# Splitting the seven-bank score visits, pairing the value products and keeping two chunks of x in a gated attention and FFN kernel

## Chip, cores and metric

The kernel runs on one core of one Trainium2 chip. The metric is the device time of one execution in microseconds (us), as the median of the timed runs. A lower time is better.

## What is computed

The program mixes two branches of the same input x (2048 tokens of 512 features, bf16) with a gate for each token. Branch a is attention with 32 heads of 16 features. The tokens are cut into four segments of 512. Inside a segment the attention is causal softmax; across segments each head carries a memory M (16 x 16) and its normaliser z. Branch b is a gated FFN of 1792 hidden features with a ReLU.

```
g = sigmoid((x * gate_w).sum(-1))
q, k, v = x@wq, x@wk, x@wv                     # 32 heads of 16
for s in range(4):                             # segments of 512 tokens
    p     = softmax(q_s k_s^T / 4 + causal mask)
    a_mem = phi(q_s) M / (phi(q_s) z + 1e-6)    # phi(t) = t+1 if t>0 else exp(t)
    o_s   = sigmoid(beta) * a_mem + (1 - sigmoid(beta)) * (p v_s)
    M, z  = M + phi(k_s)^T v_s, z + sum(phi(k_s))
a = concat(o_s) @ wo
b = (relu(x@W_gate) * (x@W_up)) @ W_down
out = g * a + (1 - g) * b
```

## The kernel before

The program is a list of small operations, made by `program`. Each has a name, an engine, the buffers it reads and writes, and a place in the list, its number. Nothing is scheduled on the chip: the table `ORDER` holds, for each of the five engines, the numbers in the order in which that engine issues them, and the string `BANKS` gives each accumulator its PSUM bank (there are eight banks of 512 float32 columns). The class `Sched` walks the table and puts a semaphore wait in front of an operation where one of its inputs, or the last reader of its bank, is on another engine. So each engine runs its own list strictly in order, and an operation that has to wait holds up all that stand behind it on the same engine.

For each segment the lists hold these steps:

- `proj`: the projections. For each of four head groups G (eight heads) and each of q and k, four matmuls over four 128-row slices of the weights are accumulated in one bank; they are issued as two operations of two slices. v is done the same way per 128 tokens. The copies out of PSUM go to VectorE or ScalarE.
- `att`: scores, exponentials, masks, value products. A block of scores is 128 rows (64 keys for each of two heads) by 512 columns; four blocks of a "quad" are made at once by matmuls of 32 rows each in four row strips of the array. A `visit` writes the blocks into PSUM, one bank for each, and ScalarE turns them into exponentials `E` in SBUF (L714); GpSimd clears what lies above the diagonal (L723). `flush` multiplies a finished head group with the values (L753, 64-row and 32-column strips of the array) into two banks, p = 0 and 1, which VectorE transposes (L761, names `tr`), scales and adds to the memory part.
- `mu` and `nd`: the update of the memory and its read-out (L629, L646, names `num`).
- `ffn`: for each of 14 hidden tiles f, gate (`wg`) and up (`wu`) matmuls, four each in two operations (L839), ReLU of the gate bank (L847 or L848, names `relu`), and the product on VectorE (L850).
- `outp`: the down projection and the output projection, accumulated in one bank for each 128 tokens (L876, L869), scaled and stored.

All weights are loaded once at the start, one slice of 128 rows for a DMA, issued by SyncE (SP) in the order of its list. The value weights wv have four slices; the operation `v0_t` for 128 tokens t of segment 0 comes in two halves, the first of which reads slices 0 and 1 and the second slices 2 and 3. In segments 1 to 3 one visit in four takes seven banks: four blocks with one exponential of 2048 columns and three blocks with one of 1536.

Two lines of the kernel say which buffers there are, and where the seven-bank visits start:

```
QTN, EKN, HTN, OTN, XR = 8, 2, 19, 6, 3
SEVEN = [(), (1,), (1,), (1,)]
```

`XR` is the number of 512-token chunks of x kept transposed in SBUF; `load_x(c)` fills slot c % XR. `QTN` counts slots of q, `HTN` tiles of the FFN's hidden layer, and `TNN` (2) the transposed float32 value products.

Of the kernel before, what the change touches and what calls it, by code (L numbers as in the profile page):

```python
# [6 lines left out]
ALU = mybir.AluOpType  # L7
# [6 lines left out]
TNN = 2  # L14
# [7 lines left out]
QTN, EKN, HTN, OTN, XR = 8, 2, 19, 6, 3  # L22
UNITS = [[8] * 18] * 4
SEVEN = [(), (1,), (1,), (1,)]
CORDER = [[(0, 1, 7, 2, 6, 3, 5, 4), (4, 1, 7, 2, 6, 3, 5, 0)] * 2] * 4
BANKS = ("701342567041527365075111110511114561100067000056077557744557776607075650067657567676454604703400205304145400746001111611"
         "222364635647607727657075506750675616500711762307015104015045015405611111671111127063677076765446007057756705650775670756"
         "10704514215041501053452000012000035766457077516654445757740675546175")
ORDER = {k: [int(x) for x in v.split()] for k, v in {
    "pe": """  # L30
# [386 lines left out]
def program(sc, nc, T, PS, A_x, A_wq, A_wk, A_wv, A_wo, A_beta, W_g, W_u, W_d, gate_w, out, NSEG, KT, NF, NT, EPS, SCALE):  # L417
# [16 lines left out]
    def act(fn, occ, **k):  # L434
        return op("act", fn, occ, **k)
# [506 lines left out]
```

## Time and profile before

| what | value |
|---|---|
| median of 3 timed runs | 261.5 us (261.03 to 261.54) |
| profiled execution: span from first to last instruction | 260.0 us |
| profiled execution: time outside its span | not on the page; the timed runs lie 1.0 to 1.5 us above the span |
| TensorE (PE) busy | 252.7 us, 97% |
| ScalarE (ACT), VectorE (DVE), GpSimd (POOL) busy | 188.0, 171.7, 121.2 us |
| granted TensorE clock | 1.000 |
| HBM read, written | 10.14 MB, 2.11 MB |

The span is one execution taken by the hardware profiler. A row of groups gives the line, engine, operation, what is written and read, the count, busy time in us and the mean ns of one instruction, then the idle time of the engine before them and what ended it. A row of the timeline gives the start and the length in us of a merged run of like instructions; SPq rows are issues of DMAs, and their landing is given apart.

### The profile page before, as it was taken

Reading aid. Unit: us, or ns where it says so; the run is one execution under the profiler, and the core shown is the slowest. Engines: PE = TensorE matmul, PEld = TensorE weight load, DVE = VectorE, ACT = ScalarE, POOL = GpSimd, SP = SyncE. Lnnn points to the kernel's source line nnn. Section 1 sums busy time; section 2 is a strip of 40 time slices with the busy share of each in tenths; the row PEclk is TensorE's granted clock in tenths of the full one; section 3 lists DMA queues with packets and bytes.
Section 4 is the critical chain, followed back from the end, with each engine's and each line's share of the span. In section 5 each row is a group of like instructions: output and inputs, shape, how many; then the busy total and the mean of one; then the engine's idle time right before and its main releaser. Section 6 shows DMA issues by size and latency. Waiting matters only on the chain.

```text
span 260.0 us, 6414 instructions
## 1 busy us (share of the span) xinstructions
PE 252.7 (97%) x2621; PEld 115.4 (44%) x2655; DVE 171.7 (66%) x342; ACT 188.0 (72%) x173; POOL 121.2 (47%) x295
## 2 busy tenths in 40 slices
PE   8999999999999999999999999999999999999997
PEld 4433443434444544444544444434444445343544
DVE  2487788778655789777834478677762138875764
ACT  4598898988778788987777666979787685787000
POOL 2014766575736372587402944257620881168100
DMA  6899997115362311422041023100023022100002
GB/s 217 244 297 221 204 171 162 59 61 143 69 151 52 64 26 37 84 42 63 3 126 42 3 42 59 28 0 0 4 45 83 15 28 43 40 4 0 3 3 81
DMA packets 34925, 19.61 MB, mean 75 GB/s; under 512 B 24144, under 2 KB 34256, under 8 KB 34896
## 3 DMA queue, kind: packets, MB, share of 16 engines
q1 hardware_dynamic: 34512, 18.80, 31.5%
q8 instruction: 21, 0.34, 0.6%
q10 hardware_dynamic: 384, 0.40, 0.4%
q14 instruction: 8, 0.07, 0.1%
HBM read 10.14 MB, written 2.11 MB: 47 GB/s over the span
## 4 chain that ended last, share of the span: by engine, by line
PE 97%; issue 2%; DVE 0%
PE ps L839 38%; PE ps L876 19%; PE ps L589 11%; PE ps L703 9%; PE ps L753 7%; PE ps L587 5%; PE ps L869 5%; PE ps L646 1%; PE ps L506 1%; PE ps L629 1%; PE ps L518 0%; PE ps L527 0%; DVE osb L884 0%
## 5 line engine op out<-in xcount | busy, mean ns | idle before, releaser
L714 ACT ACTIVATE E<-ps 128x2048 bf16<-128x2048 f32 (+1 forms) x75 | 134.3, 1808 | 35.0 <-PE ps L703 34.9
L723 POOL TENSOR_SCALAR_AFFINE_SELECT E<-E 128x256 bf16<-128x256 bf16 (+1 forms) x256 | 100.9, 422 | 103.7 <-ACT E L714 90.3
L839 PE MATMUL ps<-xT,wg 128*128 128x512 bf16 x216 | 58.7, 380 | 1.1 <-issue 0.6
L839 PE MATMUL ps<-xT,wu 128*128 128x512 bf16 x213 | 57.4, 380 | 1.6 <-issue 1.6
L876 PE MATMUL ps<-wd,hT 128*128 128x512 bf16 (+2 forms) x231 | 52.7, 366 | 0.9 <-issue 0.8
L850 DVE TENSOR_TENSOR hT<-ps,rl 128x512 bf16<-128x512 f32 x56 | 37.9, 681 | 14.7 <-PE ps L839 14.2
L876 PEld LDWEIGHTS ps<-wd,hT 128*128 128x128 bf16 x238 | 21.7, 98 | 25.0 <-issue 2.5
L839 PEld LDWEIGHTS ps<-xT,wu 128*128 128x128 bf16 x224 | 20.0, 98 | 25.5 <-issue 3.9
L839 PEld LDWEIGHTS ps<-xT,wg 128*128 128x128 bf16 x224 | 20.2, 98 | 24.5 <-issue 2.8
L884 DVE TENSOR_SCALAR osb<-ps,omg 128x512 bf16<-128x512 f32 (+2 forms) x15 | 10.6, 715 | 27.9 <-PE ps L869 23.9
L703 PE MATMUL ps<-qT,kp 32*128 32x512 bf16 (+7 forms) x512 | 27.6, 286 | 0.0
L761 DVE STREAM_TRANSPOSE Tn<-ps 128x512 f32<-128x512 f32 x32 | 21.4, 699 | 8.3 <-PE ps L753 8.2
L848 DVE TENSOR_SCALAR rl<-ps 128x512 bf16<-128x512 f32 x27 | 18.3, 684 | 9.3 <-PE ps L839 9.2
L847 ACT ACTIVATE rl<-ps 128x512 bf16<-128x512 f32 x29 | 17.1, 595 | 6.7 <-PE ps L839 6.7
L703 PEld LDWEIGHTS ps<-qT,kp 32*128 32x128 bf16 x512 | 9.1, 92 | 24.9 <-ACT E L714 9.3
L753 PE MATMUL ps<-E,vaug 64*17 64x128 bf16 (+7 forms) x512 | 18.6, 283 | 0.0
L753 PE MATMUL ps<-E,vsh 64*17 64x128 bf16 (+7 forms) x512 | 18.2, 283 | 0.0
L770 POOL TENSOR_TENSOR adT<-Tn,rdg 128x512 bf16<-128x512 f32 x12 | 12.7, 1055 | 11.7 <-DVE rdg L768 8.8
L587 PE MATMUL ps<-wv,xT 128*128 128x512 bf16 x60 | 16.6, 379 | 0.6 <-issue 0.6
L589 PE MATMUL ps<-xT,wk 128*128 128x512 bf16 x62 | 16.8, 379 | 0.1
L869 PE MATMUL ps<-wo,oT 128*128 128x512 bf16 (+2 forms) x67 | 16.1, 366 | 0.1
L589 PE MATMUL ps<-xT,wq 128*128 128x512 bf16 (+2 forms) x67 | 15.9, 367 | 0.2 <-issue 0.2
(70 smaller groups left out, 215.8 us busy)
## 6 DMA issues: line engine op xcount, KB each, us to landing
vsh<-vaug SPq DMA_DIRECT2D x8, 272.0 KB, 3.2
out_dram<-osb SPq DMA_DIRECT2D x15, 128.0 KB, 1.9
wg<-in_B_W_gate_dram SPq DMA_DIRECT2D x8, 224.0 KB, 6.1
wu<-in_B_W_up_dram SPq DMA_DIRECT2D x8, 224.0 KB, 5.2
osb<-in_A_x_dram SPq DMA_DIRECT2D x14, 128.0 KB, 3.0
wd<-in_B_W_down_dram SPq DMA_DIRECT2D x7, 256.0 KB, 3.4
wk<-in_A_wk_dram SPq DMA_DIRECT2D x4, 128.0 KB, 3.6
wv<-in_A_wv_dram SPq DMA_DIRECT2D x4, 128.0 KB, 3.6
```

The source lines that it names most:

```text
L587: ins = e.matmul(A(ep)[:, :], lhsT=V.xT[:, kt, tok + col * 128:tok + (col + 1) * 128], rhs=w[:, kt, :], start=(kt == 0), stop=(kt == KT - 1))
L589: ins = e.matmul(A(ep)[:, c0:c1], lhsT=w[:, kt, col * 128:(col + 1) * 128], rhs=V.xT[:, kt, tok + c0:tok + c1], start=(kt == 0 and c0 == 0 ...
L703: ins = q.matmul(PS[:, ep.bank + i, o:o + w], lhsT=V.kp[r, kslot(s, G), c, :], rhs=V.qT[r, qslot(s, G), q0:q0 + w], start=True, stop=True, ...
L714: return a.activation(V.E[:, n * 512:(n + k) * 512].rearrange("q (b n) -> q b n", n=512), PS[:, x.bank:x.bank + k, :], ACT.Exp, scale=SCALE)
L723: pool(lambda g, ap=ap, lim=lim: g.affine_select(out=ap, in_=ap, compare_op=ALU.is_ge, fill=0.0, base=lim, pattern=[[0, 4], [1, 64]], chan ...
L753: ins = q.matmul(A(eps[p])[32 * jj:32 * jj + 17, 64 * (c + u):64 * (c + u + n)], lhsT=v[:, 8 * G + 2 * jj + p, :], rhs=V.E[r, f:f + 64 * n ...
L761: dve(lambda e, p=p, ep=eps[p]: e.transpose(V.Tn[:, 2 * (G % (TNN // 2)) + p, :], A(ep)[:, :]), 709, writes=[f"Tn{2 * (G % (TNN // 2)) + p ...
L839: ins = e.matmul(A(ep)[:, :], lhsT=w[:, kt, f * 128:(f + 1) * 128], rhs=V.xT[:, kt, c % XR * 512:(c % XR + 1) * 512], start=(kt == 0), sto ...
L848: ("dve", lambda e, ep=eg, r=r: e.tensor_scalar(V.rl[:, r, :], A(ep)[:, :], 0.0, None, ALU.max), t_dve(512))],
L850: dve(lambda e, ep=eu, r=r, hs=hs: e.tensor_tensor(V.hT[:, hs, :], A(ep)[:, :], V.rl[:, r, :], ALU.mult), t_dve(512), reads=[f"rl{r}"], wr ...
L869: ins = e.matmul(A(ep)[:, 0:c1 - c0], lhsT=V.oT[:, ot[G], i * 128:(i + 1) * 128], rhs=V.wo[:, G, c0:c1], start=st_ and G == 0, stop=sp_ an ...
L876: ins = e.matmul(A(ep)[:, 0:c1 - c0], lhsT=V.hT[:, slots[f], i * 128:(i + 1) * 128], rhs=V.wd[:, f, c0:c1], start=st_ and f == f0, stop=sp ...
```

## The change

The constants, the buffers and the code of the visits change, and the whole table of orders and banks is another one.

```diff
-TNN = 2
+TNN = 4
-QTN, EKN, HTN, OTN, XR = 8, 2, 19, 6, 3
+QTN, EKN, HTN, OTN, XR = 6, 2, 22, 6, 2
-SEVEN = [(), (1,), (1,), (1,)]
+SEVEN = [(), (2,), (2,), (2,)]
+PAIR = (0, 9)
...
     "sp": """
-4 5 8 9 10 11 12 13 14 15 16 17 18 27 20 19 21 24 22 23 94 26 39 25 92 32 28 31 38 167 40 36 102 37 43 35 29 30 166 33 44 100 34 211 212 104 53 101
+4 5 8 9 10 11 12 13 14 15 17 18 27 20 19 16 24 21 22 90 26 23 39 25 32 88 31 38 50 28 40 98 163 37 30 29 162 35 49 33 47 34 96 45 36 208 207 44 42
...
-        ("braw", [128, 32], BF16), ("eb", [128, 32], F32), ...
+        ("eb", [128, 32], F32), ...
-        ... ("gl", [128, NT], F32), ("tq", [128, 32], BF16),
-        ("rden", [128, 64], F32), ("rdg", [128, 64], F32), ("rdm", [128, 128], F32), ...
+        ("rden", [128, 64], F32), ("rdg", [128, 64], F32), ("rdm", [128, 64], F32), ...
...
-        def visit(groups):
+        def visit(rows, cut):
+            groups = [rows[:cut], rows[cut:]] if cut else [rows]
...
-                    visits.append([[(k + 2 * i, j) for j in range(4)], rows[3 * i:3 * i + 3]])
+                    visits.append(([(k + 2 * i, j) for j in range(4)], 2))
+                    visits.append((rows[3 * i:3 * i + 3], 0))
...
-            while carry and all(left.get(x) == 0 for x in carry[0][3]):
+            while len(carry) > 1 and k in PAIR and all(left.get(x) == 0 for c in carry[:2] for x in c[3]):
+                flush()
                 flush()
```

- A seven-bank visit becomes two operations that stand next to each other on PE. The first writes four banks, and its exponential is cut into two of 1024 columns (two accumulators of two banks). The second writes three banks, with one exponential of 1536 columns. There are 75 visits in place of 63, and 87 exponentials in place of 75.
- A head group's value product is held back until the next group is finished too, and both are created together; four buffers for the transposed products in place of two.
- x keeps two chunks on chip, so that chunks 2 and 3 are loaded into the slots of chunks 0 and 1 after the last matmul that reads those.
- The raw beta is loaded into the first columns of Mbd16, the gate's sums go into gexp, and the read-out of the memory has two buffers for its denominators in place of four.

Lines from 450 on move by 2 to 5: L450 becomes L452, L587 L589, L589 L591, L629 L631, L646 L648, L703 L706, L753 L756, L839 L844, L876 L881.

The orders differ nearly everywhere. Three places follow. The first is the start of the program, on SP, which issues the loads. Numbers 15 to 18 of its table are the slices 0 to 3 of wv, 27 is the gate's weight row gwb, 19 to 22 are slices 0 to 3 of the first half of wg and 23 to 26 those of wu. A row stands for one issue or a run of like ones, and the bracket names the semaphore that SP waits for before it, here that of an earlier load which used the same semaphore. SP before, from the loads of wv on:

```order
L450 DMA wv<-in_A_wv_dram 128x512 x4
L450 DMA gwb<-in_gate_w_dram 128x512 [waits s_dma1]
L450 DMA wg<-in_B_W_gate_dram 128x896 [waits s_dma3]
L450 DMA wg<-in_B_W_gate_dram 128x896 [waits s_dma4]
L450 DMA wg<-in_B_W_gate_dram 128x896 [waits s_dma5]
L450 DMA wu<-in_B_W_up_dram 128x896 [waits s_dma6]
```

SP of the change, from the same place:

```order
L452 DMA wv<-in_A_wv_dram 128x512 x3
L452 DMA gwb<-in_gate_w_dram 128x512
L452 DMA wg<-in_B_W_gate_dram 128x896 [waits s_dma0]
L452 DMA wg<-in_B_W_gate_dram 128x896 [waits s_dma2]
L452 DMA wv<-in_A_wv_dram 128x512 [waits s_dma4]
L452 DMA wu<-in_B_W_up_dram 128x896 [waits s_dma5]
```

Slice 1 of wv moved from the second to the seventh place, behind gwb and the first two slices of wg; the other six keep their order.

On PE the first matmuls that read wv stand at another place too. PE before, from the first scores' neighbourhood (L589 with wk are the k projections, L587 those of v, L703 the scores, L839 the gate):

```order
L587 MATMUL ps<-wv,xT 128x512 [waits s_dma11,s_dma12,s_act]
L587 MATMUL ps<-wv,xT 128x512
L589 MATMUL ps<-xT,wk 128x512 x2
L587 MATMUL ps<-wv,xT 128x512 [waits s_dma13,s_dma15]
L587 MATMUL ps<-wv,xT 128x512
L589 MATMUL ps<-xT,wk 128x512 x4
L703 MATMUL ps<-qT,kp 128x512 [waits s_dve,s_act]
L703 MATMUL ps<-qT,kp 128x512 x3
L587 MATMUL ps<-wv,xT 128x512 x2
L589 MATMUL ps<-xT,wk 128x512 x2
L587 MATMUL ps<-wv,xT 128x512 x2
L839 MATMUL ps<-xT,wg 128x512 [waits s_dma3,s_dma4,s_dve]
```

PE of the change, at the same stage:

```order
L591 MATMUL ps<-xT,wq 128x512
L706 MATMUL ps<-qT,kp 128x512 [waits s_dve,s_act]
L706 MATMUL ps<-qT,kp 128x512 x3
L589 MATMUL ps<-wv,xT 128x512 [waits s_dma11,s_dma4]
L589 MATMUL ps<-wv,xT 128x512
L591 MATMUL ps<-xT,wk 128x512 x2
L589 MATMUL ps<-wv,xT 128x512 [waits s_dma12,s_dma13]
L589 MATMUL ps<-wv,xT 128x512
L589 MATMUL ps<-wv,xT 128x512 [waits s_dve]
L589 MATMUL ps<-wv,xT 128x512 x3
L844 MATMUL ps<-xT,wg 128x512 [waits s_dma0,s_dma2,s_dve]
```

The first matmul of v waits for the semaphores 11 and 4, which are those of the wv loads in the first and the seventh place above. Ahead of the first scores no v matmul is left (there were four), and two of the k matmuls have gone behind it.

The second place is in segment 1, on PE after the value product of head group 1. L753 is its last row before, L756 in the change; L646 and L648 are the read-out of the memory. Before:

```order
L753 MATMUL ps<-E,vaug 17x64 x4
L839 MATMUL ps<-xT,wg 128x512 x4
L589 MATMUL ps<-xT,wk 128x512 x4
L839 MATMUL ps<-xT,wg 128x512 x2
L839 MATMUL ps<-xT,wu 128x512 x2
L703 MATMUL ps<-qT,kp 128x384 x4
```

And in the change:

```order
L756 MATMUL ps<-E,vaug 17x64 x4
L706 MATMUL ps<-qT,kp 128x384 x4
L706 MATMUL ps<-qT,kp 128x128 x4
L844 MATMUL ps<-xT,wg 128x512 x2
L648 MATMUL ps<-Mbd,phiq 128x8x17 x4
L844 MATMUL ps<-xT,wg 128x512 x2
```

The third read-out of the memory in this segment, which writes into two banks, now follows the value product after one visit and two matmuls; one of its banks is the one from which VectorE takes the first of the two transposes `tr` of that value product.

The third place is a seven-bank visit of segment 2, on PE. Before, the visit stands among the down projection (L876) and the output projection (L869):

```order
L703 MATMUL ps<-qT,kp 128x448 [waits s_act,s_dve]
L703 MATMUL ps<-qT,kp 128x448 x3
L703 MATMUL ps<-qT,kp 128x64 x4
L703 MATMUL ps<-qT,kp 128x384 x3
L703 MATMUL ps<-qT,kp 128x128 x3
L876 MATMUL ps<-wd,hT 128x512 x6
L869 MATMUL ps<-wo,oT 128x512 [waits s_dve]
```

In the change a split visit stands between a gate and an up tile of the FFN (L844):

```order
L844 MATMUL ps<-xT,wg 128x512 [waits s_act]
L844 MATMUL ps<-xT,wg 128x512 x3
L706 MATMUL ps<-qT,kp 128x256 [waits s_dve]
L706 MATMUL ps<-qT,kp 128x256 x7
L706 MATMUL ps<-qT,kp 128x320 [waits s_act,s_dve]
L706 MATMUL ps<-qT,kp 128x448 x2
L706 MATMUL ps<-qT,kp 128x192
L706 MATMUL ps<-qT,kp 128x64 x2
L844 MATMUL ps<-xT,wu 128x512 [waits s_dve]
L844 MATMUL ps<-xT,wu 128x512 x3
```

The second half now has a wait of its own, and the up tile behind it waits for VectorE: `BANKS` gives it the bank of the gate tile that stands just ahead of the visit, so the ReLU of that tile (L848, on VectorE here) comes between the two.

More of the change, by code (lines that the diff above doesn't have):

```diff
@@ L476, in program @@
     load("sp", ["gwb"], V.gwb[:, :], gate_w.partition_broadcast(128), 1 << 17)
-    load("sp", ["braw"], V.braw[:], A_beta.partition_broadcast(128), 8192)
+    load("sp", ["braw"], V.Mbd16[:, 0, 0:32], A_beta.partition_broadcast(128), 8192)
     load_gu(1)
@@ L548, in program @@
             kept or dma("sp", lambda e, t=t, row=row: e.dma_start(row, A_x[0, t * 128:(t + 1) * 128, :]), 1 << 17, writes=rows, name=f"ldxr{t}")
-            dve(lambda e, t=t, row=row: e.tensor_tensor_reduce(out=row, in0=row, in1=V.gwb[:], scale=1.0, scalar=0.0, op0=ALU.mult, op1=ALU.add, accum_out=V.gl[:, t:t + 1]),
+            dve(lambda e, t=t, row=row: e.tensor_tensor_reduce(out=row, in0=row, in1=V.gwb[:], scale=1.0, scalar=0.0, op0=ALU.mult, op1=ALU.add, accum_out=V.gexp[:, t:t + 1]),
                                  900, reads=rows + ["gwb"], writes=rows + [f"gl{t}"], name=f"gate{t}")
-        act(lambda e, t0=t0, t1=t1, gx=gx: e.activation(gx, V.gl[:, t0:t1], ACT.Exp), 197, reads=[f"gl{t}" for t in range(t0, t1)], writes=[f"gexp{c}"], name="gexp")
+        act(lambda e, t0=t0, t1=t1, gx=gx: e.activation(gx, V.gexp[:, t0:t1], ACT.Exp), 197, reads=[f"gl{t}" for t in range(t0, t1)], writes=[f"gexp{c}"], name="gexp")
         om = V.omg[:, t0:t1]
@@ L684, in quad @@
             return base, vid, steps, diag, sorted({p[0] for p in parts})
-        def visit(groups):
+        def visit(rows, cut):
+            groups = [rows[:cut], rows[cut:]] if cut else [rows]
             eps, todo, rd = [], [], set()
-            for rows in groups:
-                ep = Epoch("main", len(rows))
+            for part in groups:
+                ep = Epoch("main", len(part))
                 eps.append(ep)
-                for i, (k, j) in enumerate(rows):
+                for i, (k, j) in enumerate(part):
                     base, vid, steps, diag, Gs = get(k)
                     for o, G, c, q0, w in steps:
-                        todo.append((o, -j, len(eps), ep, i, G, c, q0, w))
+                        todo.append((o, -j, ep, i, G, c, q0, w))
                     rd |= {f"kp{kslot(s, G)}_{h}" for G in Gs for h in range(2)} | {f"qT{qslot(s, G)}" for G in Gs}
@@ L697, in visit @@
                 x.group = eps
-            todo.sort(key=lambda x: (x[2], x[0], x[1]))
+            todo.sort(key=lambda x: (x[0], x[1]))
             def fq(q):
-                for o, j, _, ep, i, G, c, q0, w in todo:
+                for o, j, ep, i, G, c, q0, w in todo:
                     r = slice(-32 * j, 32 - 32 * j)
@@ L704, in fq @@
                 return ins
-            name = f"{s}_{get(groups[0][0][0])[4][0]}_{vctr[0]}"
+            name = f"{s}_{get(rows[0][0])[4][0]}_{vctr[0]}"
             vctr[0] += 1
-            pe(fq, len(groups) * 512 / 2.4 + 16.0, reads=sorted(rd), writes=[x.res for x in eps[1:]], name=f"quad{name}", mode="r", ep=eps[0], role="w")
-            for rows, x in zip(groups, eps):
-                blocks = [get(k)[0] + j for k, j in rows]
-                k, n = len(rows), blocks[0]
+            pe(fq, 512 / 2.4 + (2.0 if cut else 16.0), reads=sorted(rd), writes=[x.res for x in eps[1:]], name=f"quad{name}", mode="r", ep=eps[0], role="w")
+            for part, x in zip(groups, eps):
+                blocks = [get(k)[0] + j for k, j in part]
+                k, n = len(part), blocks[0]
                 assert blocks == list(range(n, n + k))
@@ L715, in visit @@
                 act(fx, t_act(k * 512), writes=[f"E{n + i}" for i in range(k)], name=f"exp{name}", ep=x, role="r")
-                for q, j in rows:
+                for q, j in part:
                     base, vid, _, diag, Gs = get(q)
@@ L801, in att @@
                 for i in range(4):
-                    visits.append([[(k + 2 * i, j) for j in range(4)], rows[3 * i:3 * i + 3]])
+                    visits.append(([(k + 2 * i, j) for j in range(4)], 2))
+                    visits.append((rows[3 * i:3 * i + 3], 0))
                 k += 7
             else:
-                visits.append([[(k, j) for j in range(4)]])
+                visits.append(([(k, j) for j in range(4)], 0))
                 k += 1
-        for n, v in enumerate(visits):
-            k = v[0][0][0]
+        for n, (rows, cut) in enumerate(visits):
+            k = rows[0][0]
             if k in SEVEN[s]:
@@ L812, in att @@
                     get(q)
-            visit(v)
-            for q in sorted({k for rows in v for k, _ in rows}):
+            visit(rows, cut)
+            for q in sorted({k for k, _ in rows}):
                 for G in quads[q][1]:
```

34 lines of the change are left out of this document (17 added, 17 removed), and 81 rows, old and new, of the table ORDER.

## Prediction

> **What bounds the kernel now.** I read the page first, then the granted clock, the waits of PE, and the timeline of the first 16 us.
>
> ```profile
> span 260.0 us, 6414 instructions
> PE 252.7 (97%) x2621; PEld 115.4 (44%) x2655; DVE 171.7 (66%) x342; ACT 188.0 (72%) x173; POOL 121.2 (47%) x295
> PE 97%; issue 2%; DVE 0%
> core 0: 260.0 us, clock 1.000
> PE ps L839 <- DVE hT L850: 0.2, 1, 0.2
> ```
>
> PE is busy 97% of the span at the full clock, the chain that ended last is PE from end to end, and its waits for other engines are of the size of the last row: 0.2 us in all, once. There is no slack to recover on PE: the time is the sum of its work, and each new wait of PE lengthens the run by its own length. So two questions decide: does PE's own work shrink, and does the new order make PE wait?
>
> **The start, where PE runs close behind the loads.** PE from 10 us on (start, length, both in us):
>
> ```profile
> 10.05 0.59 PE L587 MATMUL ps<-wv,xT 128*128 128x512 bf16 x2
> 10.48 0.59 PE L589 MATMUL ps<-xT,wk 128*128 128x512 bf16 x2
> 10.92 0.59 PE L587 MATMUL ps<-wv,xT 128*128 128x512 bf16 x2
> 11.35 1.03 PE L589 MATMUL ps<-xT,wk 128*128 128x512 bf16 x4
> 12.31 0.39 PE L703 MATMUL ps<-qT,kp 32*128 32x512 bf16 x4
> 12.63 0.60 PE L587 MATMUL ps<-wv,xT 128*128 128x512 bf16 x2
> 13.08 0.59 PE L589 MATMUL ps<-xT,wk 128*128 128x512 bf16 x2
> 13.51 0.59 PE L587 MATMUL ps<-wv,xT 128*128 128x512 bf16 x2
> 14.13 1.02 PE L839 MATMUL ps<-xT,wg 128*128 128x512 bf16 x4
> ```
>
> The loads by tile, each with its issue times (first and last) and the us from issue to landing: the four of wv, gwb, the first two of wg, the fourth of wg, and the wu load issued at 11.6:
>
> ```profile
> L450 SPq DMA_DIRECT2D wv<-in_A_wv_dram x4: 432/432/432, 5.0 to 6.5; - x4
> DMA to landing us min/median/max: 3.5/3.6/4.2
> ...
> L450 SPq DMA_DIRECT2D gwb<-in_gate_w_dram x1: 430/430/430, 6.9 to 6.9; - x1
> DMA to landing us min/median/max: 5.9/5.9/5.9
> ...
> L450 SPq DMA_DIRECT2D wg<-in_B_W_gate_dram x2: 430/430/430, 7.4 to 7.9; - x2
> DMA to landing us min/median/max: 6.0/6.1/6.2
> ...
> L450 SPq DMA_DIRECT2D wg<-in_B_W_gate_dram x1: 552/552/552, 9.3 to 9.3; - x1
> DMA to landing us min/median/max: 6.5/6.5/6.5
> ...
> L450 SPq DMA_DIRECT2D wu<-in_B_W_up_dram x1: 548/548/548, 11.6 to 11.6; - x1
> DMA to landing us min/median/max: 5.8/5.8/5.8
> ```
>
> The wv slices land between 8.7 (5.0 + 3.7) and 10.7 (6.5 + 4.2), gwb at 12.8, the two wg slices at 13.4 and 14.1. From issue to landing the time grows from 3.6 to over 6 us: from gwb on the loads queue behind each other and land in the order of issue. A matmul row starts 0.43 us after the one before for two matmuls (0.216 each), so the v matmuls at 13.51 are through at 13.94, and L839 starts at 14.13, when its second wg slice has landed: a wait of 0.19 us.
>
> **The late slice of wv (one term, +2.6 us).** Of the seven loads from wv to the second wg slice, slice 1 is now issued last instead of second. The seven are the same as before, and the last of them landed at 14.1 us. So slice 1 lands at about 14.1 instead of 9.1 (some 5.5 + 3.6). PE's first v matmul reads slices 0 and 1 and stands right behind the first scores. Before, the first scores ended at 12.63, with two v pairs and one more k pair ahead of them that now come later: PE is there at 12.63 - 3 x 0.43 = 11.3. It waits until 14.13, which is 2.8 us, in place of 0.19. Counted the other way: by 14.13 PE had done the four v pairs (10.05, 10.92, 12.63, 13.51) and two more k pairs (11.78, in the row at 11.35, and 13.08); in the new order these six stand behind the wait. 6 x 0.43 = 2.6 us. Everything queued behind this operation on PE is late by that, and nothing later in the program gives it back, since PE has no idle time. What PE does before 11.3 us doesn't matter; a different order there is covered by the wait. The loads after the seventh keep nearly their places, and PE, 2.6 us later, comes to them with more margin than before.
>
> A rule on this queue: the Trainium skill, "DMA: Bandwidth & Descriptors", section "Queues, rings and completion order", says that descriptors on each DMA engine are consumed in ring order, though a later transfer may complete before an earlier one. By ring order the term stands at 2.6; the rows above agree, with landings in issue order, and no row here shows a transfer overtaking.
>
> **Two new waits in the middle (+0.5 us).** How soon VectorE frees a bank, and what PE needs to come back:
>
> ```profile
> L761 DVE STREAM_TRANSPOSE Tn<-ps 128x512 f32<-128x512 f32 x32 | 21.4, 699 | 8.3 <-PE ps L753 8.2
> 49.23 0.20 PE L753 MATMUL ps<-E,vaug 64*17 64x64 bf16 x4
> 49.55 1.31 DVE L761 STREAM_TRANSPOSE Tn<-ps 128x512 f32<-128x512 f32 x2
> ...
> 15.09 0.40 PE L703 MATMUL ps<-qT,kp 32*128 32x448 bf16 x8
> 15.42 0.60 PE L839 MATMUL ps<-xT,wg 128*128 128x512 bf16 x2
> ...
> 16.29 1.46 PE L839 MATMUL ps<-xT,wg 128*128 128x512 bf16 x6
> 16.92 0.69 DVE L848 TENSOR_SCALAR rl<-ps 128x512 bf16<-128x512 f32 x1 [1.05 <-PE ps L839]
> ...
> 74.56 0.61 PE L703 MATMUL ps<-qT,kp 32*128 32x448 bf16 x14
> 75.11 1.04 PE L876 MATMUL ps<-wd,hT 128*128 128x512 bf16 x4
> ```
>
> Segment 1, read-out behind the value product: the first transpose starts 0.32 us after the last value matmuls start (49.23 to 49.55) and takes 0.70; PE starts about 0.09 after a release (the wg slice at 14.0 to 14.1, L839 at 14.13). The bank is usable 1.11 us after 49.23. PE gets there after the rest of these short matmuls and the change to the visit's strips (0.15), the visit (0.33 from 15.09 to 15.42) and two matmuls (0.43): 0.91. A wait of 0.20. Segment 2, the up tile behind the split visit: the ReLU starts 0.42 after the gate tile's last matmul starts (16.50, the second of the row at 16.29, to 16.92) and takes 0.69; with 0.09 the bank is ready after 1.20. PE needs 0.216, 0.10 to enter the strips, and 0.55 for the seven banks (74.56 to 75.11): 0.87. A wait of 0.33. I followed the other waits of PE in the same way and found none over 0.1 us. A dozen or so, mostly at the start of a visit, end within 0.1 us of PE's arrival, where PE is changing its tiling anyway (0.10 to 0.12, next part); I take them as hidden, and as a rival otherwise.
>
> **PE's own work (-0.1 us).** The matmuls are the same in number and size. PE changes its kind of work (whole array, row strips, column strips) 145 times in the order before and 141 times now. Entering strips costs 0.10 (L839 through at 14.99, L703 at 15.09), leaving them 0.11 (eight score matmuls are 0.213 long, from 15.09 to 15.30; L839 at 15.42), so four fewer are worth -0.3 to -0.4. Splitting a seven-bank visit adds a boundary. No row shows two score visits in a row. Bounds: nothing, as inside the visit at 74.56, whose seven banks take 0.55 = 2 x 0.213 + 0.11; at most another entry of 0.10, so 12 x 0.10 = 1.2 us. The nearest row is the pair of value products that stands back to back in this kernel:
>
> ```profile
> 242.91 0.46 PE L753 MATMUL ps<-E,vaug 64*17 64x64 bf16 x8
> 242.99 0.57 PE L753 MATMUL ps<-E,vsh 64*17 64x512 bf16 x8
> ```
>
> The second starts in the same row in which the first ends, without a gap, so I take 12 x 0.02 = 0.2 us. Together about -0.1, with ends of -0.4 and +0.9.
>
> **What costs nothing.** Splitting 12 exponentials adds 12 ACT instructions. The two sizes of before, and the loads that transpose x (us to landing; an issue):
>
> ```profile
> L714 ACT ACTIVATE E<-ps 128x2048 bf16<-128x2048 f32 x63 | 118.2, 1876 | 26.7 <-PE ps L703 26.6
> L714 ACT ACTIVATE E<-ps 128x1536 bf16<-128x1536 f32 x12 | 17.4, 1449 | 8.3 <-PE ps L703 8.3
> ...
> xT<-in_A_x_dram SPq DMA_TRANSPOSE x12, 3.4
> 12.14 1.24 SPq L454 DMA_TRANSPOSE xT<-in_A_x_dram  x1
> ```
>
> 512 columns cost 0.43 us, so the fixed part is 0.17 and ACT gains 12 x 0.17 = 2.0 us of work. It idles 35 us before these rows; without that cover the 2.0 us would come on top. Two chunks of x on chip: chunk 3 can be loaded only after the last gate or up matmul of segment 1. Its last transposing load stands on SP behind a vsh load that waits for the segment's last value product. Behind that wait SP issues four more (an estimate of 0.4 to 1.2 us each, at most 4) before this one lands 3.4 us later, 7.4 at most, against some 40 matmuls (8.7 us) on PE until the first v matmul of segment 3: a margin of over 1 us; if that is gone, it costs what it is late. Four transposed buffers, shorter rings of q and denominators, the hidden tiles and the moved beta change no path that ends last.
>
> **Sum.** 260.0 + 2.6 + 0.5 - 0.1 = 263.0 us of span. The timed median is 1.5 above the span of the profiled execution, so 264.5 us.
>
> **Rivals.**
> - *Slice 1 lands in time* (0.09). If loads could overtake, it would land 3.6 us after its issue at 7.9, at 11.5, and PE would wait only 0.3 (11.3 to 11.6). Against it: gwb and wg, issued around it, took 5.9 to 6.2. Then PE comes early to the weights behind. After five pairs (v, k, v, v, v), a wg pair, a visit of 0.43 with its changes, a k and a wg pair it needs wg slice 3, still the tenth load, at 15.5; that lands at 15.8 (9.3 + 6.5), and PE starts at 15.9: 0.4 lost. Two pairs later, at 16.75, it needs the first slice of wu, now the thirteenth load, and the thirteenth landed at 17.4 (11.6 + 5.8): 0.7 lost. In all 1.4 less the 0.19 of before, 1.2 us; with the +0.4 of the other terms 261.5 + 1.6 = 263.1.
> - *Not slower* (0.03): the weights land ahead of PE everywhere, and the two banks are free in time, so that only the fewer changes of tiling remain: 261.5 - 0.4 = 261.1. The point that decides is whether slice 1 lands by 11.3 us and the first wu slice by 16.7; the queue's rows at 12.8, 14.1 and 17.4 speak against it.
> - *The hidden waits are not hidden* (0.10): if a change of tiling runs only after the wait, about 16 places cost 0.11 each, 1.8 us: 266.3. Nothing in this trace shows such a pair.
> - *PE loses its clock in the gap* (0.05). A cold matmul is seen at the start:
>
> ```profile
> L506 PE MATMUL ps<-const-bfloat16-1.0 128*128 128x512 bf16 (+1 forms) x9 | 2.7, 486 | 0.8 <-PEq L927 0.8
> ```
>
>   Five of 512 and four of 128 columns take 2.7 us, about twice the warm rate. If a gap of 2.8 us put PE back to that rate for as long as these took, half of 2.7 us would be lost: 264.5 + 1.4 = 265.9. The granted clock is 1.000 throughout and no gap here is long enough to tell. The Trainium skill, "TensorE: Matmul & The Clock Gate", "Part 1: The HAM clock gate", has the clock halved after at least one idle window of about 3.4 us; by that rule this gap is too short, and the time stays as forecast.
>
> **Numbers.** The likeliest case (0.73) is 264.5, by itself 263.8 to 265.3 (the landing's 0.4, the split's ends). The range 263.0 to 266.2 holds it and the times of the first and the last rival; the third lies on its edge. A change under 0.2% (0.5 us) can't be told from none here. Slower 0.95, same 0.03, faster 0.02.
>
> **What would show it.** In the new profile PE should idle some 2.8 us until about 14.1 in front of the first v matmul (L589 there), released by the DMA of wv; a wait of 0.2 us before L648 and one of 0.3 before L844 in segments 1 and 2; PE busy unchanged; score visits in a row without a gap; a full clock. If wv's last load lands near 11.5, the main term is wrong. If PE's waits for ACT and DVE come to more than 1 us, the hidden ones weren't.

## The result, and the profile after

The change makes the kernel slower, as forecast: 264.12 us (median of 6, 263.48 to 266.65) against 261.32 (median of 6, 261.03 to 261.54), a ratio of 1.0118 with a 95% interval of 1.0086 to 1.015. The forecast was 264.5. The profiled execution took 263.63 us; its span is 262.4, 2.4 above that of before, where 3.0 was forecast. Two of the six runs show a granted clock of 0.994 and are the two slowest, 265.28 and 266.65. So the median sits near the forecast partly by luck: the terms came to 0.6 less than forecast and the time outside the span to 1.2 instead of 1.5, while some runs lost clock, which the forecast left out. In the repeat of this kernel and in the run with the filler, both below, the profiled execution was a disturbed one (296.42 and 664.80 us), so neither its trace nor its time is used.

From the page of after: span, busy time, the chain that ended last by engine, and from the view of cores the clock:

```profile
span 262.4 us, 6451 instructions
PE 258.1 (98%) x2655; PEld 116.4 (44%) x2655; DVE 171.8 (65%) x348; ACT 186.7 (71%) x179; POOL 120.5 (46%) x295
PE 94%; SPq 2%; DMA 2%; DVE 0%; issue 0%
core 0: 262.4 us, clock 1.000
```

A DMA queue and a DMA now stand on the chain; before it was PE alone. PE's busy time of 258.1 can't be set against the 252.7 of before, where the trace holds 34 matmuls less (2621 records for the 2655 that after's trace has in full); its own work is worked out from start times instead. The waits of PE (us in all, times, longest) and the loads of wv (issue times and landing, as before):

```profile
PE ps L589 <- DMA wv<-in_A_wv_dram: 1.1, 1, 1.1
PE ps L844 <- DVE rl L853: 0.2, 1, 0.2
PE ps L520 <- DMA hT<-in_A_x_dram: 0.2, 1, 0.2
```

```profile
L452 SPq DMA_DIRECT2D wv<-in_A_wv_dram x4: 430/432/432, 5.0 to 7.9; - x4
DMA to landing us min/median/max: 3.1/3.7/5.7
```

And PE's timeline around the wait:

```profile
9.67 2.32 PE L591 MATMUL ps<-xT,wk 128*128 128x512 bf16 x10
11.83 0.38 PE L591 MATMUL ps<-xT,wq 128*128 128x512 bf16 x1
12.14 0.40 PE L706 MATMUL ps<-qT,kp 32*128 32x512 bf16 x4
13.67 0.60 PE L589 MATMUL ps<-wv,xT 128*128 128x512 bf16 x2 [1.13 <-DMA wv<-in_A_wv_dram]
14.11 0.59 PE L591 MATMUL ps<-xT,wk 128*128 128x512 bf16 x2
```

The last wv load is issued at 7.9, takes 5.7 us, lands at 13.6, and the first v matmul follows at once. The wait shown is 1.1 us and not 2.8, since PE got there at 12.5 instead of 11.3: it began its transposes 0.37 later (3.73, not 3.36) and ran at its cold rate for longer in this execution (below); and the load landed at 13.6, not 14.1. What is lost does not depend on that: six pairs of matmuls, 2.59 us, stand behind 13.67 that before were done by 14.13, so 2.59 - 0.46 = 2.13.

The two waits in the middle, segment 1 and segment 2:

```profile
104.37 0.20 PE L756 MATMUL ps<-E,vaug 64*17 64x64 bf16 x4
104.50 0.40 PE L706 MATMUL ps<-qT,kp 32*128 32x384 bf16 x8
104.69 1.31 DVE L764 STREAM_TRANSPOSE Tn<-ps 128x512 f32<-128x512 f32 x2 [0.49 <-PE ps L756]
104.83 0.60 PE L844 MATMUL ps<-xT,wg 128*128 128x512 bf16 x2
105.46 0.43 PE L648 MATMUL ps<-Mbd,phiq 128*128 128x136 bf16 x4
...
144.01 1.03 PE L844 MATMUL ps<-xT,wg 128*128 128x512 bf16 x4
144.97 0.62 PE L706 MATMUL ps<-qT,kp 32*128 32x256 bf16 x14
145.08 0.69 DVE L853 TENSOR_SCALAR rl<-ps 128x512 bf16<-128x512 f32 x1
145.83 1.04 PE L844 MATMUL ps<-xT,wu 128*128 128x512 bf16 x4 [0.24 <-DVE rl L853]
```

Two gate matmuls from 104.83 are through at 105.26, and L648 starts at 105.46: 0.20. The transpose started 0.32 after the last value matmuls, as in the trace of before. The up tile at 145.83 stands behind a visit from 144.97 that takes 0.55 for seven banks, so it could have started at 145.52: 0.31. The row at 144.97 holds both parts of a split visit, 14 matmuls in one row without a gap.

From 13.67 to the end there are 248.73 us. Less the six pairs (2.59) and the two waits (0.51) that is 245.63, against 245.87 from 14.13 to the end before: PE's own work is 0.24 shorter. 2.13 + 0.51 - 0.24 = 2.40, the difference between the spans. This sum closes by the way it is made, for the 0.24 is what is left over. Two things speak for it from outside. After's trace holds all its matmuls, and behind 9 us only three gaps between their starts exceed the matmul's own length by more than 0.14 us: the one at 13.67 and these two. And the same 0.24 closes the sums of five other kernels (below, under "What bounds the kernel").

### The profile page after: what moved, and what is told of

Read it like the earlier page. It is cut to its first block, busy times and chain, and to the rows that moved or that the text cites. A ratio compares the mean times of both kernels' runs of the same rounds, so it can differ in the third digit from the quotient of the medians.

```text
span 262.4 us, 6451 instructions
## 1 busy us (share of the span) xinstructions
PE 258.1 (98%) x2655; PEld 116.4 (44%) x2655; DVE 171.8 (65%) x348; ACT 186.7 (71%) x179; POOL 120.5 (46%) x295
## 4 chain that ended last, share of the span: by engine, by line
PE 94%; SPq 2%; DMA 2%; DVE 0%; issue 0%
PE ps L844 38%; PE ps L881 19%; PE ps L591 9%; PE ps L706 9%; PE ps L756 7%; PE ps L589 5%; PE ps L874 5%; SPq L452 2%; DMA wv<-in_A_wv_dram 2%; PE ps L648 1%; PE ps L631 1%; DVE rl L853 0%; DVE osb L889 0%
## 5 line engine op out<-in xcount | busy, mean ns | idle before, releaser
L717 ACT ACTIVATE E<-ps 128x2048 bf16<-128x2048 f32 (+2 forms) x87 | 135.3, 1582 | 32.8 <-PE ps L706 32.3
L726 POOL TENSOR_SCALAR_AFFINE_SELECT E<-E 64x256 bf16<-64x256 bf16 (+1 forms) x256 | 99.6, 419 | 100.2 <-ACT E L717 89.8
L844 PE MATMUL ps<-xT,wu 128*128 128x512 bf16 x224 | 60.5, 380 | 0.2 <-DVE rl L853 0.2
L844 PE MATMUL ps<-xT,wg 128*128 128x512 bf16 x224 | 59.9, 380 | 0.0
L881 PE MATMUL ps<-wd,hT 128*128 128x512 bf16 (+2 forms) x238 | 56.2, 367 | 0.0
L881 PEld LDWEIGHTS ps<-wd,hT 128*128 128x128 bf16 x238 | 21.4, 98 | 24.8 <-issue 2.8
L844 PEld LDWEIGHTS ps<-xT,wg 128*128 128x128 bf16 x224 | 20.6, 98 | 24.9 <-issue 1.9
L844 PEld LDWEIGHTS ps<-xT,wu 128*128 128x128 bf16 x224 | 19.9, 98 | 25.8 <-issue 3.4
L706 PE MATMUL ps<-qT,kp 32*128 32x320 bf16 (+7 forms) x512 | 27.6, 286 | 0.0
L773 POOL TENSOR_TENSOR adT<-Tn,rdg 128x512 bf16<-128x512 f32 x12 | 13.1, 1095 | 20.4 <-DVE rdg L771 8.8
L706 PEld LDWEIGHTS ps<-qT,kp 32*128 32x128 bf16 x512 | 9.1, 92 | 24.2 <-ACT E L717 8.1
L589 PE MATMUL ps<-wv,xT 128*128 128x512 bf16 x64 | 17.4, 380 | 1.1 <-DMA wv<-in_A_wv_dram 1.1
L756 PE MATMUL ps<-E,vaug 64*17 64x128 bf16 (+7 forms) x512 | 18.2, 283 | 0.0
L756 PE MATMUL ps<-E,vsh 64*17 64x128 bf16 (+7 forms) x512 | 17.8, 283 | 0.0
L591 PE MATMUL ps<-xT,wk 128*128 128x512 bf16 x64 | 17.8, 380 | 0.0
L591 PE MATMUL ps<-xT,wq 128*128 128x512 bf16 (+2 forms) x68 | 17.6, 377 | 0.0
L889 DVE TENSOR_SCALAR osb<-ps,omg 128x512 bf16<-128x512 f32 (+1 forms) x10 | 7.1, 710 | 15.6 <-PE ps L874 15.6
L890 ACT ACTIVATE osb<-ps,omg 128x512 bf16<-128x512 f32 (+1 forms) x7 | 4.7, 672 | 16.5 <-PE ps L874 16.0
```

The costliest lines, as they stand in the source:

```text
L589: ins = e.matmul(A(ep)[:, :], lhsT=V.xT[:, kt, tok + col * 128:tok + (col + 1) * 128], rhs=w[:, kt, :], start=(kt == 0), stop=(kt == KT - 1))
L591: ins = e.matmul(A(ep)[:, c0:c1], lhsT=w[:, kt, col * 128:(col + 1) * 128], rhs=V.xT[:, kt, tok + c0:tok + c1], start=(kt == 0 and c0 == 0 ...
L706: ins = q.matmul(PS[:, ep.bank + i, o:o + w], lhsT=V.kp[r, kslot(s, G), c, :], rhs=V.qT[r, qslot(s, G), q0:q0 + w], start=True, stop=True, ...
L717: return a.activation(V.E[:, n * 512:(n + k) * 512].rearrange("q (b n) -> q b n", n=512), PS[:, x.bank:x.bank + k, :], ACT.Exp, scale=SCALE)
L726: pool(lambda g, ap=ap, lim=lim: g.affine_select(out=ap, in_=ap, compare_op=ALU.is_ge, fill=0.0, base=lim, pattern=[[0, 4], [1, 64]], chan ...
L756: ins = q.matmul(A(eps[p])[32 * jj:32 * jj + 17, 64 * (c + u):64 * (c + u + n)], lhsT=v[:, 8 * G + 2 * jj + p, :], rhs=V.E[r, f:f + 64 * n ...
```

## The experiments

All were timed in three groups, each with its own runs of the kernel before: 261.21, 261.32 and 261.39 us in the median. Every one of the 51 runs of before in these groups shows a clock of 1.000. The numbers in the lists of SP are those of the front: 15 to 18 wv, 27 gwb, 19 to 22 wg, 23 to 26 wu.

**After, again.** The kernel unchanged.

> The changed kernel once more, beside its variants. The theory (slice 1 of wv lands late, PE waits for it): most executions 2.3 to 2.8 us above the kernel before. Two of the six earlier executions had a granted clock of 0.994 and took 265.3 and 266.7 us in place of 263.5 to 264.3. If the idle gap in front of the first v matmul now and then costs PE its clock, some of these executions should again show a clock under 1 and lie 1.5 to 3 us higher, while the kernel before, which has no such gap, never does. If the lower clock is an accident of that hour, none or both kernels show it.

Measured: 264.31, ratio 1.0107 (1.0079 to 1.0135). Runs: 263.37, 263.54, 263.57, 265.05 at the full clock, 265.51 at 0.994. Three of the five are 2.2 to 2.4 above the kernel before, at the lower end of the expectation or just below it. With the first six, three of eleven are at 0.994. The run of 265.05 is high at a clock of 1.000, and no trace says why.

**Slice 1 second again.** After, with only this moved:

```diff
-12 13 14 15 17 18 27 20 19 16 24 21 22 90 26 23
+12 13 14 15 16 17 18 27 20 19 24 21 22 90 26 23
```

> The changed kernel with slice 1 of wv issued second again, gwb and all else in the order of the change. Theory: the wait for wv goes, but PE then reaches the first slice of wu, the thirteenth load, before it lands (about 17.0 us) and waits some 0.6 us there, so only 1.2 to 1.6 us of the 2.6 come back: 262.0 to 262.6 where the changed kernel has 263.5. Rival, that the loss sits in the many small waits of the middle or in the split visits: no change, 263.5. Rival, that the whole start-up loss is this one slice: 2.1 us back, 261.4.

Measured: 263.36 (262.55 to 264.72), ratio 1.0079 (1.0055 to 1.0103); the profiled run is the fastest, span 261.3. No clock below 1.000. The wait for wv is gone, and PE runs into the next load:

```profile
17.32 0.60 PE L844 MATMUL ps<-xT,wu 128*128 128x512 bf16 x2 [0.53 <-DMA wu<-in_B_W_up_dram]
```

The profiled run fits the expectation, the median is 0.8 above its upper end and by itself nearer to the first rival (no change, 263.5); that rival falls by the trace, in which the wait for wv is gone, and by the repeat of after beside it, 0.95 slower. So moving the slice gives back only part, and a second wait stands behind the first. Why these six runs spread over 2.2 us at the full clock was not traced.

**All weights early.** After with wv in order, gwb behind four slices of wg and two of wu, and the other two of wu next to it:

```diff
-15 17 18 27 20 19 16 24 21 22 90 26 23 39 25 32 88
+15 16 17 18 20 19 21 22 24 23 27 26 25 90 39 32 88
```

> The changed kernel with slice 1 second and the first halves of wg and wu in the order in which PE needs them, gwb behind slice 3 of wg. Theory: no wait for weights is left at the start, so all of the start-up loss is undone and what remains of the change is +0.5 us (two waits in the middle) and -0.3 us (fewer changes of tiling): 0.1 to 0.4 us above the kernel before, no execution with a clock under 1. Rival, that something else in the new order costs: 1 us or more above the kernel before. Rival, that the change gains once it is fed: 0.5 us or more below it.

Measured: 263.94 (262.68 to 264.87), ratio 1.0096 (1.0072 to 1.012). The expectation missed; the time is that of the first rival, that something else in the new order costs 1 us or more. PE starts the first v pair at 12.14 where 11.3 was to be had. It has no wait for weights up to 30 us, and a new one at 34:

```profile
34.77 0.61 PE L844 MATMUL ps<-xT,wu 128*128 128x512 bf16 x2 [1.27 <-DMA wu<-in_B_W_up_dram]
```

That is the half slice of wu that SP issues last (36). It is issued at 28.2 and lands at 34.7. This is not the work of the moved gwb: in after it is issued at 28.4 and lands at 34.3, and PE, late by the wait for wv, comes for it only at 34.86. In the kernel before it was issued at 20.4 and landed at 23.7. The change itself had moved it back, and the wait for wv hid that.

**The start as before, and slice 1 second.** As the run with slice 1 second, with ACT's first entries in the order of before (3 is the table load, 6 a 256 KB load of x, 7 a load of wq):

```diff
 "act":
-6 7 3 68 76 70 80
+3 6 7 68 76 70 80
```

> The kernel after with slice 1 of wv issued second again and with ACT issuing its loads at the start in the order of before (table load and small loads ahead of the 256 KB load). Theory (the later landing of the first x columns kept PE at its cold rate, and that was hidden by the wait for wv in after and shows when that wait is gone): first scores and projections start as in before, at about 3.4 us; left are the two waits in the middle, 0.5, and about 0.5 at the first slice of wu; 261.9 to 262.4, and the spread of the runs shrinks to about that of before. Rival (ACT's order has no part): as the run that moved the slice alone, 263.2 to 263.6, with its spread of 2 us.

Measured: 263.13 (262.60 to 264.04), ratio 1.0068 (1.0053 to 1.0083). Missed, by 0.7 in the median; the rival's 263.2 to 263.6 is nearer. In its profile PE starts its transposes at 3.36 as before, and what it gains it waits out at wu loads:

```profile
16.81 0.61 PE L844 MATMUL ps<-xT,wu 128*128 128x512 bf16 x2 [0.41 <-DMA wu<-in_B_W_up_dram]
...
32.53 1.02 PE L844 MATMUL ps<-xT,wu 128*128 128x512 bf16 x4 [0.52 <-DVE ek L575]
...
35.27 0.61 PE L844 MATMUL ps<-xT,wu 128*128 128x512 bf16 x2 [1.28 <-DMA wu<-in_B_W_up_dram]
```

The row in the middle names VectorE, but a half slice of wu (issued at 26.5, 5.9 us to its landing) lands at 32.4, just ahead of it. By the starts of the matmuls the three waits cost 0.58, 0.58 and 1.44 us.

**Fed in order.** ACT's order of before, wv second, the wu slices in the order of use and the last half of wu (36) ahead of the load that waits for the gates (96):

```diff
-15 17 18 27 20 19 16 24 21 22 90 26 23 39 25
+15 16 17 18 27 20 19 21 22 24 23 90 26 25 39
...
-47 34 96 45 36 208
+47 34 36 96 45 208
```

> The kernel after with both: ACT's order of before, and the weights issued in the order in which PE needs them (wv second, wu slices ahead of the second wg halves, the second half of the last wu slice ahead of the load that waits for the gates). Theory: no wait for weights is left at the start, only the two waits in the middle (0.5 us) against 0.3 less of PE's own work, so 0.1 to 0.5 above before, 261.3 to 261.8. Rival 1 (splitting the visits costs PE about 0.1 us at each of some 16 hidden waits or 12 boundaries): 1.2 us or more above before, 262.4 to 263.0. Rival 2 (a new late load takes the place of the old one): a wait for wu or wg of over 0.5 us at the start, and 262 or more.

Measured: 262.58 (262.22 to 263.38), ratio 1.005 (1.0035 to 1.0066); profiled run 262.22, span 261.0. Above the theory's range, inside that of the first rival. Waits of PE in its trace:

```profile
PE ps L844 <- issue: 0.3, 1, 0.3
PE ps L844 <- DVE rl L853: 0.2, 1, 0.2
```

No wait for a weight is named. The row with 0.3 is a gap that begins at 31.9 us, in front of an up tile that starts at 32.18; its wu slice (issued at 26.9, 5.2 us to its landing) lands at 32.1. So in this execution 0.35 is a late load after all, 0.52 the two waits in the middle, and 0.25 is saved: 0.6 of the 1.0 between the spans. The other 0.4 is the start: 0.6 for a longer cold phase (until about 5.7 us here, 4.0 in the profile of before, by the spacing of the matmuls), less the 0.19 at 14.1 that is gone.

**The wu slices ahead of two wd loads as well.**

```diff
-30 29 162 35 49 33 47 34 36 96 45
+30 29 162 35 33 34 36 49 47 96 45
```

> As the run with the weights fed in order and ACT's order of before (262.6), with the last two wu loads also ahead of two wd loads. Theory: the wait of 0.35 us at 32 us goes and nothing else, 262.0 to 262.4; the profile shows no wait of PE for a DMA over 0.1 us, and the two in the middle, 0.20 and 0.32, as the only waits over 0.1 us behind 10 us. Rival (the rest over before is a cost of the split visits spread over the program): 262.4 to 262.8, and PE's work summed outside its waits is longer than in before.

Measured: 262.16 (261.48 to 263.48, 12 runs), ratio 1.0031 (1.0014 to 1.0048). The median is in the theory's range, but its reading of the trace fails: the wait at 32 us is gone and a new one stands at 41.8, in an execution of 262.96 us.

```profile
39.79 0.59 PE L844 MATMUL ps<-xT,wu 128*128 128x512 bf16 x2
41.78 1.04 PE L844 MATMUL ps<-xT,wg 128*128 128x512 bf16 x4 [1.39 <-DVE Tn L764]
...
40.39 0.69 DVE L551 CUSTOM_DVE_ANT_0 osb<-osb,gwb 128x512 bf16<-128x512 bf16 x1 [2.97 <-DMA osb<-in_A_x_dram]
41.01 1.31 DVE L764 STREAM_TRANSPOSE Tn<-ps 128x512 f32<-128x512 f32 x2
```

VectorE's list has a gate sum (L551) in front of the transpose that frees PE's bank. Its x rows come late, and it holds the transpose for a value product that PE had finished at 39.1. The two matmuls from 39.79 are through at 40.22, so the wait costs 1.56. With 0.51 in the middle, less 0.24 of PE's own work and less the 0.19 at 14.1 that before had, that is 1.64 of the 1.7 between the spans (261.7 and 260.0). So no cost of the split itself is left over, and the rival of this run falls, with the first rival of the last one. The fastest of the 12 runs, 261.48, is 0.09 above the median of before.

**Slice 1 seventh in the kernel before.** The one change of the main term, alone:

```diff
-13 14 15 16 17 18 27 20 19 21 24 22
+13 14 15 17 18 27 20 19 16 21 24 22
```

> The kernel before with one thing moved: the second slice of wv is issued seventh on SP instead of second. Theory (loads of this queue land in issue order, and the late slice is the whole main term): it lands at 13.4 to 14.2 us, PE waits 2.9 to 3.6 us at the first v matmul (10.05 before), and the median is 2.6 to 3.4 us above before, 263.8 to 264.6; the two waits in the middle (0.20 and 0.33 in after) are absent. Rival 1 (a load issued behind others overtakes them): it lands 3.6 us after its issue, at 11.5, and the median is 1.0 to 1.6 above before, 262.2 to 262.8. Rival 2 (the gap sometimes costs PE its clock for a while): as the theory, but some runs show a granted clock of 0.994 and stand 1.5 to 3 us higher.

Measured: 265.67 (264.10 to 266.50), ratio 1.0159 (1.013 to 1.0188). The rival of an overtaking load falls; the wait is as the theory has it, and the time as the second rival has it:

```profile
14.27 0.60 PE L587 MATMUL ps<-wv,xT 128*128 128x512 bf16 x2 [3.25 <-DMA wv<-in_A_wv_dram]
```

The load landed 6.3 us after its issue. This pair started at 10.05 before: 4.22 later, less the 0.19 at 14.1 that is gone, is 4.03, and the spans differ by 4.0 (264.0). The runs at the full clock are 264.10 to 265.28, two of the three above the theory's 264.6: from 10.05 to a landing at 14.2 is more than the wait of 2.9 to 3.6 that it took, and the trace shows a wait of 3.25 only because PE came to it about 1.0 late. Three of six runs are at 0.994, and they are 266.05 to 266.50.

**Slice 1 later still.** After, with the slice eight places further back in SP's list:

```diff
-15 17 18 27 20 19 16 24 21 22 90 26 23 39 25 32
+15 17 18 27 20 19 24 21 22 90 26 23 39 25 16 32
```

> The kernel after with slice 1 of wv issued later still, behind the first slices of wg and wu, so that PE's gap in front of the first v matmul is made longer. Theory (a wait costs its own length): slice 1 lands at 17 to 18.5 us, PE waits about 5 to 6.5 us there, and the time is 3.5 to 4.8 us above that of after, 267.6 to 268.9. Rival (a gap makes PE lose its clock): a gap of this length does so in every run, the granted clock of all runs is below 1.0 and the time is another 1.4 to 3 us higher, 269.3 to 272.

Measured: 270.05 (269.16 to 271.18), ratio 1.0337 (1.0313 to 1.0361); three of five runs at a clock of 0.987, two at 0.981. The rival that a gap costs PE its clock is right. Windows of 1 us around the start and the end of the slower clock (start and end, sum, busy us of PE, PEld, DVE, ACT, POOL with their counts, then the granted clock, DMA share and GB/s):

```profile
14.00:15.00 1.00, 0.00 (x0) 0.00 (x0) 0.00 (x0) 0.00 (x0) 0.00 (x0) 0.77 1.36 377
15.00:16.00 1.00, 0.00 (x0) 0.00 (x0) 0.00 (x0) 0.00 (x0) 0.00 (x0) 0.50 1.43 204
...
20.00:21.00 1.00, 1.00 (x4) 0.42 (x3) 0.00 (x0) 0.00 (x0) 0.00 (x0) 0.50 1.15 271
21.00:22.00 1.00, 1.00 (x6) 0.39 (x4) 0.94 (x3) 0.00 (x0) 0.00 (x0) 0.82 0.00 0
```

And PE on its timeline:

```profile
11.33 0.39 PE L706 MATMUL ps<-qT,kp 32*128 32x512 bf16 x4
18.29 1.03 PE L589 MATMUL ps<-wv,xT 128*128 128x512 bf16 x2 [6.57 <-DMA wv<-in_A_wv_dram]
19.11 1.06 PE L591 MATMUL ps<-xT,wk 128*128 128x512 bf16 x2
```

PE goes idle at 11.7. The clock is halved from 14.54 (0.77 in that window) to 21.36 (0.82), 6.8 us; a pair of matmuls takes 0.82 to 0.85 instead of 0.43. From 18.29 on that loses 1.5 us: the first v matmul is 4.62 later than in after and the span is 6.1 longer. The halving begins 2.8 us after the last matmul, so PE need not be idle longer than that.

**After with ACT's order of before.** The edit of ACT's list above, alone.

> The kernel after with ACT's list at the start in the order of before. Theory (whatever PE does ahead of the wait for wv is covered by it): the runs at a full granted clock take the same as after, 263.4 to 264.4; PE comes to the wait up to 0.4 us earlier, so the gap is longer and at least as many runs as in after (3 of 11) show a clock of 0.994 and stand 1.3 to 2.6 us higher. Rival (the later start of PE is part of the loss): 0.4 to 1.0 below after, 263.0 to 263.8, at the full clock.

Measured: 264.31 (263.38 to 265.38), ratio 1.0117 (1.0088 to 1.0146): the same as after, which fits that the wait for wv covers what PE does ahead of it. It is no sharp test: in its profile PE reaches the first scores at 12.13, in after at 12.14. Four runs are at the full clock (263.38, 263.56, 263.61, 265.00), two at 0.994 (265.28, 265.38).

**The gap filled.** After with five matmuls of no use between the first scores and the first v matmul:

```diff
-... 171 168 203 191 181
+... 171 168 203 1515 191 181
...
+    fep = Epoch("att")
+    def ffill(e):
+        for i in range(5):
+            ins = e.matmul(A(fep)[:, 0:512], lhsT=V.wk[:, 0, 0:128], rhs=V.wk[:, 1, :], start=True, stop=True)
+        return ins
+    pe(ffill, 5 * 216.0, reads=["wk0", "wk1"], name="fill0", ep=fep, role="w")
```

> The changed kernel with five extra matmuls of 512 columns (1.1 us, their results are overwritten) between the first scores and the first v matmul, inside the wait. Theory of the late slice: the time of undisturbed executions doesn't move (263.3 to 263.8), since the wait is shortened by what the fillers take. If the gap is what costs the clock in some executions, its idle part is now under 1.5 us and no execution shows a clock under 1. If the lower clock has another cause, it shows up as often as in the changed kernel itself.

Measured: 264.24 (263.57 to 265.08), ratio 1.0107 (1.0088 to 1.0127), and all five runs at the full clock. At 5 in 17 for a lower clock, five runs without one would still come up with a chance of 0.18: no proof by itself. The median is above the expected 263.3 to 263.8, and next to that of after beside it (264.31), as it should be if the fillers stand in the wait; no trace shows that they do.

**Before with ACT's order of after.** The ACT edit the other way round.

> The kernel before with ACT's list at the start in the order of after (the 256 KB load ahead of the table load). Theory (the first x columns land 0.4 us later and PE starts that much later, while the length of its cold phase differs from run to run by itself): 0.2 to 0.5 above before, 261.5 to 261.8. Rival (that order makes the cold phase longer in every run): 0.8 to 1.4 above before, 262.1 to 262.7.

Measured: 261.75 (261.12 to 262.29, 12 runs), ratio 1.0008 (0.9996 to 1.0021). In the theory's range, but not told from nothing. The rival, a longer cold phase in every run, falls.

**Before with gwb behind the first wg slices.** A try at a better kernel:

```diff
-15 16 17 18 27 20 19 21 24 22 23
+15 16 17 18 20 19 21 22 27 24 23
```

> The kernel before with the load of gwb behind the first wg slices, which takes away its wait of 0.19 us at 14.1. Theory: at most 0.2 faster, 261.0 to 261.4, which the runs can hardly tell from before. Rival (with that wait gone the length of the cold phase at the start shows in full): the runs spread wider, by over 1 us, around 261.0 to 261.6.

Measured: 261.39 (260.95 to 262.07, 12 runs), ratio 1.0 (0.9987 to 1.0012). The wait of 0.19 at 14.1 is worth nothing that can be measured. No version beat the kernel before.

## Why the prediction was right, point by point

- *What bounds the kernel.* Right. PE was the sum, and each wait put in its way came out at the end in full: the slice moved in the kernel before lengthened it by what its row shows. The row given as PE's one wait, 0.2 us, was no wait: 34 matmuls are missing in that trace, and a missing one of 0.216 us looks like a wait of 0.2. The one real gap over 0.14 us behind 9 us is the 0.19 at 14.13. For the kernels without the wait for wv a sum can be made that has nothing left to fit: how much later than 11.3 us PE starts the first v pair, plus the late weights (in the run with wu first, the wait at 41.8 instead), plus 0.51, less 0.24, less 0.19. It gives 1.3, 2.3, 2.8, 1.0 and 1.7 for slice 1 second, all weights early, the start as before, fed in order and wu first; the spans are 1.3, 2.3, 2.8, 1.0 and 1.7 above that of before.
- *The late slice (+2.6).* The mechanism is right: loads of this queue land in the order of issue, and six pairs of matmuls stand behind the wait. The size was 2.1 in the profile. The landing was put at that of before's seventh load, 14.1; the slice landed at 13.6 in after, 13.4 in after with the other ACT order, and 14.2 in the kernel before. What makes up this 0.8 was not traced further. "What PE does before 11.3 us doesn't matter" held: the forecast wait of 2.8 was 1.1 in the trace, as PE was late by 1.2 in the same stretch and the load 0.5 early, and only the 0.5 shows in the span.
- *"PE comes to them with more margin than before"* held with the slice late. But "the loads after the seventh keep nearly their places" was not so for one of them, the half slice of wu that lands at 34.3 instead of 23.7. The wait hid the loads behind it: with slice 1 second, PE waited at 17 us; with the first wu slices issued earlier, at 34; with those mended, at 32 and then, through VectorE, at 42. That, and a longer cold start (0.4 in the trace of slice 1 second) that the wait had covered, is why undoing the one move that costs 2.1 gave back 0.95 in the median.
- *Two waits in the middle (+0.5).* 0.20 and 0.31 against 0.20 and 0.33, and the same in every profile of a kernel with the new order of PE.
- *PE's own work (-0.1).* -0.24, as what is left over. The split boundary was taken as 0.02 for each of 12; the rows show none, and without that term the forecast would have been -0.3 to -0.4. What the other 0.1 is stays open.
- *What costs nothing.* The 12 exponentials, the two chunks of x and the buffers show no wait of PE.
- *The rivals.* "Slice 1 lands in time" fell with the slice moved in the kernel before. "The hidden waits are not hidden" fell: such a place would show as a gap of over 0.2 us, and after's trace has only the three named. "PE loses its clock in the gap" was given 0.05 and as one case for the whole kernel; it is a case for single runs. The 12 runs of after and of after with the other ACT order at the full clock have a mean of 263.9, the five at 0.994 one of 265.6: 1.75 more, where the rival said 1.4. Two of those 12, 265.00 and 265.05, are nearly as high as those at 0.994; a clock of 1.000 does not exclude a loss there, as seven of the 14 traces hold no entry of the clock at all and are printed as 1.000. By the gap's length, runs with a lower clock: none of the 60 runs of the seven kernels without this wait, none of 51 of before in these groups; five of 17 with the gap of after (2.2 us at most by the profiles: the slice lands at 13.6, and the earliest that PE reached the first v matmul in this order is 11.4); three of six with 3.25; five of five with 6.6.

The rule cited for that rival, the Trainium skill, "TensorE: Matmul & The Clock Gate", "Part 1: The HAM clock gate", halves the clock after at least one idle window of about 3.4 us, and says that the window is free-running. The measurement goes further: a halving began 2.8 us after PE went idle, and gaps of about 2.2 us at most go with a lower clock in five of 17 runs. That the window is free-running, the clock entries in the traces bear out: in each of the seven that have them, all changes of the clock are whole multiples of 3.413 us apart (here 10.24 and 6.83 us; in after's trace 256.00), counted from a first change that differs from 3.7 to 6.7 us. A window need not be idle throughout: the one that ended with the halving at 14.54 held PE's work up to 11.7, while one with 1.7 us idle in the run of slice 1 seventh (9.35 to 12.76) passed. So a gap of 2.2 us would count or not by how it falls on the windows, which fits that only some runs lose it. One window at half clock is 0.5 x 3.413 = 1.7 us, or 0.006 of the span, so a mean of 0.994 is one window, 0.987 two and 0.981 three, and 1.7 is near the measured 1.75. In after itself no trace caught a halving; that it sits at this gap is concluded from the counts and this size.

## What to carry to other kernels

Where PE's work is the time, a load that moves back in its queue costs the landing of the place to which it moves, less what PE can do without it, and the first wait hides those behind it: before undoing one move, look for the next load that PE would catch up with. Here an idle stretch of PE of about 2 to 3 us cost more than its length in part of the runs, so read the clock of every run, not only that of the profiled one. In both places here a bank was wanted again 0.9 us after its last matmul, with a VectorE operation of 0.7 us between that left it free after 1.1 to 1.2 us. Such a wait of 0.2 to 0.3 us can be read off before anything is run.

## What the runs showed of the hardware that was not expected

The cold phase at the start ends at another time in each execution, and ACT's order of loads does not set it. The second row of x transposes (L520) in four profiles, of after, of slice 1 second, of the run fed in order and of that with wu first; four matmuls of 128 columns take 0.63 cold and 0.40 warm:

```profile
4.77 0.63 PE L520 MATMUL ps<-ident,hT 128*128 128x128 bf16 x4
```

```profile
4.46 0.40 PE L520 MATMUL ps<-ident,hT 128*128 128x128 bf16 x4
```

```profile
4.56 0.63 PE L520 MATMUL ps<-ident,hT 128*128 128x128 bf16 x4
```

```profile
4.39 0.40 PE L520 MATMUL ps<-ident,hT 128*128 128x128 bf16 x4
```

The first two have ACT's order of after, the last two that of before; in each order one is cold and one warm. The granted clock is printed as 1.000 in these rows all the same: a trace's first clock entry stands where the full clock begins (6.58 us in after, 5.72 in the run fed in order), and what lies ahead of it counts as full. So the cold start has to be read from the spacing of matmuls, 0.107 us for 128 columns against 0.056. From the earliest end seen (3.7 us, in the start as before with slice 1 second) to the latest (6.7, in after with ACT's order of before) the half rate costs at most half of 3.0, 1.5 us. That spread belongs to the execution and not to the kernel, and the start of one profile is no measure of an order.
